# First unit's row maxima in two pairs, its loads ahead of two seed stores, and a third tile for evacuating q and k

## The chip, the cores and the metric

One core of one Trainium2 chip runs the whole program. The metric is the device time of one execution in microseconds, as the median of several runs; one further execution was recorded by the profiler, and all rows below are from that one.

## The reference

Two independent layers work on two inputs and their results stand side by side in the output (2048 rows, 448 + 448 columns).

```python
# A: a long convolution (S4D): kernel K from 256 complex modes per channel, applied by FFT
dt = exp(log_dt); A = -exp(log_A_real) + 1j * A_imag; C = (C_real + 1j * C_imag) * dt[:, None]
P = exp((A * dt[:, None])[:, :, None] * arange(2048))
K = 2.0 * einsum("dn,dnl->dl", C, P).real              # 448 channels
y = irfft(rfft(u, 4096) * rfft(K, 4096), 4096)[:2048] + u * D_skip
# B: full multi-head attention, 16 heads of 28, no mask
q, k, v = split_heads(x @ wqkv)                         # 2048 x 448 each
p = softmax(q @ k^T * 28 ** -0.5)                       # row maximum over all 2048 keys
b = (p @ v) @ wo
out = concatenate([y, b], axis=-1)
```

## The kernel before

The program has a first part of some 240 us and a long main loop. A wrapper records every instruction, so all instructions have line 75 in the profile, and one goes by tile names.

**First part.** Queries, keys and values are projected from `x` in four chunks `c` of 512 rows. `qk_proj(c, s, g)` computes keys (`s == 1`) or queries (`s == 0`) of a group `g` of four heads by 12 matmuls into one of three PSUM tiles `pm`. Its `evac` splits the result into a high part (ScalarE) and a low part (VectorE) in a tile `hl` (two buffers), and stores that to DRAM (`k_d`, `q_d`). The weights lie in the tile `khat` (`k0_t`) of the first group's keys, a quarter of the tile for each group of heads, so a quarter can be loaded with keys when its group's last projection is done. `work` holds the projections, `project()` emits one and the evacuation of the one before it.

Between the projections lie the seeds of layer A: for each of eight blocks `o` a list of 13 steps, `seeds(o)`, four slots apart, up to slot 41. They make the tables `se` (in a buffer of the ring `qhat`, three buffers, shared with the loaded queries) and `sg`. The steps that matter here, in their order: `sizes` (11 exponentials, ScalarE), `reduce` (VectorE), `sines` (ScalarE), `g_base` (GpSimd and ScalarE, tile `gz`), `places`/`e_base` (GpSimd, tile `qhat`), `e3` and `g_first` (VectorE), `e5` (GpSimd, six operations with `x_e`), `g_copies` (ScalarE), and two stores, `put_g` (1456 KB) and `put_e` (896 KB), from `sg` and `qhat` to `sd`.

Then come the row maxima of the first unit, 512 queries of four heads: 16 row tiles `i`, of each four matmuls against 512 columns. Columns 0 to 1023 are handled as a pair: `kdif` holds key differences of the two halves, ScalarE takes relu(q kdif) into `rl`, and VectorE adds the product with the second half and reduces to the maximum in one instruction (`tensor_tensor_reduce`, in the profile CUSTOM_DVE_ANT_0 and a short read). Columns 1024 to 2047 are two plain maxima (TENSOR_REDUCE). `max_join` and `max_end` join the maxima and transpose them, and `max_put` writes the negated maximum (tile `mh`) by two small DMAs into the rows 28 and 29 of the queries, where the main loop's scores take it as an added row.

**Order.** In the first part a scheduler orders each engine's instructions from emission order and its own costs; from the main loop on the emission order is kept. All loads and stores are issued from SyncE, in one order: an instruction that waits there holds all that follow. Each waits for the one eight places before it.

**Main loop.** It begins with three row tiles of the second unit's maxima (`LEAD = 3`, 12 matmuls), then steps through 256 steps: scores `pss`, exponential `p`, product with `v`, next maxima, the convolution's work in slots.

What the change touches: `A1` and `KW` (slots in which the loads of the first queries and keys are emitted), `hl`, `project()`, `max_mm`'s callers, `max_join`, the two last steps of `seeds(6)`.

Of the kernel before, what the change touches and what calls it, by code (L numbers as in the profile page):

```python
# [23 lines left out]
HG = H // G  # L24
CQ = 512
NQ = L // CQ
# [14 lines left out]
PS = 1  # L41
SGB, XB, XL = 2, 5, 4
K0, KP, KD, UP = 0, 3.5, 4, 3
A0, A1, KW = 26, 34, (33, 35, 36)

N1 = 32
N2 = 64
# [5 lines left out]
NO = 8  # L53
# [37 lines left out]
def body(ctx, tc, a, out):  # L91
    nc = Engines(tc)
# [39 lines left out]
    kd_p = pool(att, "kd_p", side="right")  # L132
    k0_p = pool(k0_st, "k0_p", side="right")
# [31 lines left out]
    def load_q(u, rows=range(4)):  # L165
        g, c = divmod(u, NQ)
        if 0 in rows:
            q_u[u] = q_p.tile([128, HG, CQ], F32R, name="qhat", bufs=3)
        t = q_u[u]
        for r in rows:  # L170
            nc.sync.dma_start(t[32 * r:32 * r + 32].bitcast(F32), q_d[g][c][r // 2].rearrange("(j p) q -> p j q", j=HG))

    def max_mm(u, i, kc, ps=w_tile):

        if i == 0 and kc == 0:
            m_u[u] = q_p.tile([128, HG, 4, 3], F32, name="mx", bufs=2)
        j, t = divmod(i, 4)
        pm = ps()
        q, kt = q_u[u][:, j, t * 128:(t + 1) * 128], kt_g[u // NQ][j]
        mx = m_u[u][:, j, t, max(kc - 1, 0):max(kc - 1, 0) + 1]  # L180
        if kc == 0:
            nc.tensor.matmul(pm, q, kd_g[u // NQ, j], start=True, stop=True)
            rl_u[u, i] = kd_p.tile([128, CQ], F32, name="rl", bufs=2)
            nc.scalar.activation(rl_u[u, i], pm, AF.Relu)
        elif kc == 1:
            kb = kt.rearrange("p (c s n) -> p c s n", c=NQ, s=2)[:, :2, 1, :]
            nc.tensor.matmul(pm.rearrange("p (c n) -> p c n", c=2), q, kb, start=True, stop=True)
            rl = rl_u.pop((u, i))
            nc.vector.tensor_tensor_reduce(rl, pm, rl, 1.0, -3.0e38, ALU.add, ALU.max, mx)
        else:  # L190
            nc.tensor.matmul(pm, q, kt[:, kc * CQ:(kc + 1) * CQ], start=True, stop=True)
            nc.vector.tensor_reduce(mx, pm, axis=AX.X, op=ALU.max)

    def max_join(u):
        m_u[u, 1] = q_p.tile([128, HG * 4], F32, name="m1", bufs=2)
        nc.vector.tensor_reduce(m_u[u, 1], m_u[u].rearrange("p a b c -> p (a b) c"), axis=AX.X, op=ALU.max)

    def max_end(u, ps):
        nc.tensor.transpose(ps[:16, :128], m_u[u, 1], ident)
        mh = q_p.tile([16, 2, 128], F32R, name="mh")  # L200
        nc.vector.tensor_scalar(mh[:, 0, :], ps[:16, :128], -1.0, None, op0=ALU.mult)
        nc.vector.scalar_tensor_tensor(mh[:, 1, :], ps[:16, :128], -1.0, mh[:, 0, :].bitcast(F32),
                                       op0=ALU.mult, op1=ALU.subtract)
        mh_u[u] = mh
# [7 lines left out]
    with ExitStack() as st:  # L212
# [3 lines left out]
        x_p = pool(xst, "x_p")  # L216
# [43 lines left out]
        t = a["A_log_dt"]  # L260
# [197 lines left out]
        def qk_proj(c, s, g):  # L458
            pp = w_tile()
            n = 0  # L460
            for k in range(NCK):
                for i, x_ in ((0, xh), (1, xh), (0, xl)):
                    nc.tensor.matmul(pp, w_g[:, i, s, k, g].rearrange("p h e -> p (h e)"), x_[k],
                                     start=n == 0, stop=n == 3 * NCK - 1)
                    n += 1

            def evac():
                hl = x_p.tile([128, 2, CQ], F32R, name="hl", bufs=2)
                th, tl = hl[:, 0], hl[:, 1]
                if s == 1:  # L470
                    nc.scalar.activation(th, pp, AF.Identity, bias=kones)
                    nc.vector.scalar_tensor_tensor(tl, pp, kones, th.bitcast(F32), op0=ALU.add, op1=ALU.subtract)
                else:
                    nc.scalar.activation(th, pp, AF.Copy)
                    nc.vector.tensor_tensor(tl, pp, th.bitcast(F32), ALU.subtract)
                if s == 1 and c < 2:
                    HC = CQ // 2
                    kb = y_p.tile([128, HC], F32, name="kb")
                    dhl = y_p.tile([128, 2, HC], F32R, name="dhl")
                    dh, dl = dhl[:, 0], dhl[:, 1]  # L480
                    nc.scalar.activation(kb, pp[:, HC:], AF.Copy)
                    nc.vector.tensor_tensor(kb, pp[:, :HC], kb, ALU.subtract)
                    nc.scalar.activation(dh, kb, AF.Copy)
                    nc.gpsimd.tensor_tensor(dl, kb, dh.bitcast(F32), ALU.subtract)
                    nc.sync.dma_start(kd_d[g][:, :, c * HC:(c + 1) * HC].rearrange("i p l -> p i l"), dhl.bitcast(F32))
                nc.sync.dma_start((k_d[g][:, :, c * CQ:(c + 1) * CQ] if s == 1 else q_d[g][c]).rearrange("i p l -> p i l"),
                                  hl.bitcast(F32))
            return evac
# [16 lines left out]
        work = []  # L505
# [8 lines left out]
        stages = [seeds(o) for o in range(NO)]  # L514
        n_stage = SP * (NO - 1) + len(stages[0])
        slots = [[] for _ in range(n_stage)]
        for o in range(NO):
            for i, st_ in enumerate(stages[o]):
                slots[max(SP * o + (i or -2), 0)] += st_
# [3 lines left out]
        ahead = collections.defaultdict(list)  # L523
# [2 lines left out]
        for i in range(2):  # L526
            ahead[A1 + i].append(lambda i=i: load_q(0, range(2 * i, 2 * i + 2)))

        for j, t in enumerate(KW):
            ahead[t].append(lambda j=j: load_k(0, j, k0_p))  # L530

        def project():

            e = work.pop(0)() if work else None
            while pend:
                pend.pop(0)()
            if e:
                pend.append(e)

        for t in range(n_stage):  # L540
            while work and n_work - len(work) < n_work * (t + 1) / PW:
                project()
            for f in slots[t] + ahead.get(t, []):
                f()
            if t + 1 == PW:
                project()
                wst.close()
                load_k(0, HG - 1, k0_p)
                load_q(1)
                for c in range(NQ):  # L550
                    load_v(0, c)
        xst.close()
        more = [lambda: ps_t.tile([128, CQ], F32, name="pt")] * 2 + [w_tile] * 3
        for i in range(16):
            for kc in range(4):
                max_mm(0, i, kc, more[(4 * i + kc) % 5])
        nc.scalar.activation(half_pi[:1], half_pi[:1], AF.Exp)
        max_join(0)
        max_end(0, ps_t.tile([128, CQ], F32, name="pt"))
        max_put(0)  # L560
        sst.close()
# [315 lines left out]
    for i in range(LEAD):  # L877
        for kc in range(4):
            max_mm(1, i, kc)
# [122 lines left out]
    last = [None]  # L1002
# [13 lines left out]
    for s in range(NS):  # L1016
        u, kt = divmod(s, NK)
# [24 lines left out]
        ps = []  # L1042
# [97 lines left out]
```

## Time and profile before

| | |
|---|---|
| median of 3 runs | 1292.87 us (1292.81 to 1293.53) |
| profiled execution, its time | 1296.34 us |
| its span, first to last instruction | 1294.3 us |
| mean granted TensorE clock | 0.976 |
| TensorE busy | 1228.1 us (95%) |
| VectorE, ScalarE, GpSimd busy | 933.2, 956.6, 847.0 us |
| moved by DMA | 205.36 MB, 159 GB/s on the mean |

The profiled execution is 3.5 us longer than the median run. Shares over the whole span say little of the first part; what the change touches runs in the first 250 us.

### The profile page before, as it was taken

Reading aid. Unit: us, or ns where it says so; the run is one execution under the profiler, and the core shown is the slowest. Engines: PE = TensorE matmul, PEld = TensorE weight load, DVE = VectorE, ACT = ScalarE, POOL = GpSimd, SP = SyncE. Lnnn points to the kernel's source line nnn. Section 1 sums busy time; section 2 is a strip of 40 time slices with the busy share of each in tenths; the row PEclk is TensorE's granted clock in tenths of the full one; section 3 lists DMA queues with packets and bytes.
Section 4 is the critical chain, followed back from the end, with each engine's and each line's share of the span. In section 5 each row is a group of like instructions: output and inputs, shape, how many; then the busy total and the mean of one; then the engine's idle time right before and its main releaser. Section 6 shows DMA issues by size and latency. Waiting matters only on the chain.

```text
span 1294.3 us, 33256 instructions
## 1 busy us (share of the span) xinstructions
PE 1228.1 (95%) x12625; PEld 703.1 (54%) x12625; DVE 933.2 (72%) x2106; ACT 956.6 (74%) x2142; POOL 847.0 (65%) x728
## 2 busy tenths in 40 slices
PE   7979885899999999999999999999999999999997
PEld 5767762455555555555555555555555555554433
DVE  5778876878777787787788888888888655645111
ACT  4878762488888888888888888888887766656552
POOL 2466571398888788888769999998996222424321
PEclk9889887899999999999999999999999999999999
DMA  6677779736765546468634132742425443647655
GB/s 193 229 261 253 245 235 289 210 73 145 181 147 137 125 139 166 131 164 237 177 95 111 48 87 52 164 108 68 103 51 155 154 152 133 202 151 243 201 163 169
DMA packets 200088, 205.36 MB, mean 159 GB/s; under 512 B 95992, under 2 KB 158520, under 8 KB 197880
## 3 DMA queue, kind: packets, MB, share of 16 engines
q1 hardware_dynamic: 199928, 203.23, 55.7%
q8 instruction: 100, 1.64, 0.5%
q14 instruction: 60, 0.49, 0.1%
HBM read 120.73 MB, written 82.18 MB: 157 GB/s over the span
## 4 chain that ended last, share of the span: by engine, by line
PE 76%; DVE 9%; POOL 5%; ACT 4%; issue 3%; DMA 3%; SPq 0%; ACTq 0%; POOLq 0%; DVEq 0%
PE pm L75 43%; PE pss L75 16%; PE po L75 16%; DVE mx L75 2%; ACT tri L75 1%; POOL e L75 1%; DVE rl L75 1%; DMA khat<-k 1%; POOL qhat L75 1%; DVE tri L75 1%; DVE px L75 1%; DVE sg L75 1%; DVE qhat L75 1%; POOL p L75 1%; PE pt L75 1%
## 5 line engine op out<-in xcount | busy, mean ns | idle before, releaser
L75 ACT ACTIVATE p<-pss 128x512 f32<-128x512 f32 x1024 | 561.2, 611 | 112.1 <-PE pss L75 107.6
L75 PE MATMUL pss<-qhat,khat 128*128 128x512 f32 x1024 | 403.1, 400 | 1.5 <-ACT p L75 1.4
L75 DVE TENSOR_REDUCE mx<-pm 128x1 f32<-128x512 f32 x500 | 321.7, 684 | 109.2 <-PE pm L75 107.0
L75 PE MATMUL pm<-khat,qhat 128*128 128x512 f32 x749 | 327.1, 440 | 3.3 <-DVE mx L75 2.1
L75 POOL TENSOR_TENSOR e<-e,sdb 128x256 f32<-128x256 f32 x168 | 201.9, 1202 | 118.6 <-ACT e L75 109.3
L75 PE MATMUL po<-p,v 128*32 128x512 f32 x2048 | 269.4, 594 | 0.0
L75 POOL TENSOR_TENSOR e<-e,eu 128x256 f32<-128x256 f32 x168 | 248.1, 1477 | 13.2
L75 PEld LDWEIGHTS pm<-khat,qhat 128*128 128x128 f32 x749 | 141.9, 190 | 199.1 <-ACT p L75 48.6
L75 DVE CUSTOM_DVE_ANT_0 rl<-pm,rl 128x512 f32<-128x512 f32 x249 | 171.5, 689 | 65.6 <-ACT rl L75 62.0
L75 PEld LDWEIGHTS pss<-qhat,khat 128*128 128x128 f32 x1024 | 190.7, 189 | 45.7 <-issue 10.8
L75 POOL TENSOR_TENSOR eu<-e,sdb 128x256 f32<-128x256 f32 x168 | 201.9, 1202 | 0.0
L75 POOL TENSOR_TENSOR p<-pr,pr 64x448 f32<-64x448 f32 x64 | 73.1, 1143 | 159.5 <-PE pm L75 134.0
L75 ACT ACTIVATE rl<-pm 128x512 f32<-128x512 f32 x249 | 151.2, 607 | 20.9 <-PE pm L75 20.9
L75 DVE TENSOR_TENSOR g<-g,zg 128x128 f32<-128x128 f32 x392 | 162.2, 414 | 3.4
L75 PE MATMUL pm<-xh,khat 112*128 112x512 f32 x256 | 90.3, 434 | 14.1 <-DVE hl L75 7.1
L75 PE MATMUL pm<-kdif,qhat 128*128 128x512 f32 x249 | 101.3, 407 | 2.4 <-DVE mx L75 1.3
L75 DVE TENSOR_TENSOR zg<-g,zg 128x128 f32<-128x128 f32 x224 | 87.9, 393 | 5.1
L75 PEld LDWEIGHTS pm<-e,g 128*32 128x32 f32 x3584 | 57.2, 109 | 43.8 <-issue 16.4
L75 DVE TENSOR_TENSOR pr<-pm,ub 128x448 f32<-128x448 f32 x64 | 37.0, 620 | 56.4 <-PE pm L75 42.0
L75 PE MATMUL pm<-e,g 128*32 128x64 f32 x3584 | 73.0, 222 | 1.9 <-POOL e L75 1.9
L75 ACT ACTIVATE y<-pm 128x448 f32<-128x448 f32 x48 | 26.5, 553 | 58.1 <-PE pm L75 34.0
L75 PEld LDWEIGHTS pm<-xh,khat 112*128 112x128 f32 x256 | 52.5, 209 | 29.0 <-DVE hl L75 8.6
(134 smaller groups left out, 1446.0 us busy)
## 6 DMA issues: line engine op xcount, KB each, us to landing
sdb<-sd SPq DMA_DIRECT2D x56, 336.0 KB
khat<-k SPq DMA_DIRECT2D x64, 256.0 KB
qhat<-q SPq DMA_DIRECT2D x64, 256.0 KB
sd<-sg SPq DMA_DIRECT2D x8, 1456.0 KB
k<-hl SPq DMA_DIRECT2D x16, 512.0 KB
q<-hl SPq DMA_DIRECT2D x16, 512.0 KB
mw<-in_mw SPq DMA_DIRECT2D x16, 512.0 KB
sd<-qhat SPq DMA_DIRECT2D x8, 896.0 KB
```

The costliest lines, as they stand in the source:

```text
L75: i = f(*args, **kw)
```

## The change

For columns 1024 to 2047 of the first unit, the two plain maxima become a second pair: TensorE adds q k2 and (-q) k3 in one PSUM tile (two matmuls), ScalarE takes the relu, and VectorE adds q k3 and reduces, as for the first pair. The negated queries `q_neg` are four ScalarE instructions of 128x512. Per row tile there are five matmuls instead of four, two ScalarE instructions instead of one, two VectorE pairs instead of one pair and two maxima.

The queries' load is emitted three slots earlier, the keys' loads inside `project()`. The stores `put_g` and `put_e` of `seeds(6)` are taken out of their slots: `put_e` is emitted behind the last keys' load and one load of values, `put_g` behind the loads of the second unit's queries and the other values. `hl` has three buffers.

```diff
-A0, A1, KW = 26, 34, (33, 35, 36)
+A0, A1 = 26, 31
+    def max_pair(i, kc, ps, q_neg):
+        j, t = divmod(i, 4)
+        ts = slice(t * 128, (t + 1) * 128)
+        pm, kt = ps(), kt_g[0][j]
+        if kc == 2:
+            nc.tensor.matmul(pm, q_u[0][:, j, ts], kt[:, 2 * CQ:3 * CQ], start=True, stop=False)
+            nc.tensor.matmul(pm, q_neg[:, j, ts], kt[:, 3 * CQ:], start=False, stop=True)
+            rl_u[0, i] = kd_p.tile([128, CQ], F32, name="rl", bufs=2)
+            nc.scalar.activation(rl_u[0, i], pm, AF.Relu)
+        else:
+            nc.tensor.matmul(pm, q_u[0][:, j, ts], kt[:, 3 * CQ:], start=True, stop=True)
+            rl = rl_u.pop((0, i))
+            nc.vector.tensor_tensor_reduce(rl, pm, rl, 1.0, -3.0e38, ALU.add, ALU.max, m_u[0][:, j, t, 1:2])
-    def max_join(u):
+    def max_join(u, n=3):
...
-                hl = x_p.tile([128, 2, CQ], F32R, name="hl", bufs=2)
+                hl = x_p.tile([128, 2, CQ], F32R, name="hl", bufs=3)
...
+        kept_g, kept_e = (stages[NO - 2][i] for i in (-2, -1))
+        stages[NO - 2][-2:] = []
...
-        for j, t in enumerate(KW):
-            ahead[t].append(lambda j=j: load_k(0, j, k0_p))
         def project():
-            e = work.pop(0)() if work else None
+            j, last = divmod(len(work) - 1, 2)
+            e = work.pop(0)() if work else load_k(0, HG - 1, k0_p)
             while pend:
                 pend.pop(0)()
             if e:
                 pend.append(e)
+            if e and not last and j < HG - 1:
+                load_k(0, HG - 2 - j, k0_p)
...
             if t + 1 == PW:
                 project()
                 wst.close()
-                load_k(0, HG - 1, k0_p)
+                load_v(0, 0)
+                kept_e.pop()()
                 load_q(1)
-                for c in range(NQ):
+                for c in range(1, NQ):
                     load_v(0, c)
+                kept_g.pop()()
...
+        q_neg = pool(n_st, "n_p").tile([128, HG, CQ], F32R, name="q_neg")
+        for j in range(HG):
+            nc.scalar.activation(q_neg[:, j], q_u[0][:, j].bitcast(F32), AF.Copy, scale=-1.0)
         for i in range(16):
             for kc in range(4):
-                max_mm(0, i, kc, more[(4 * i + kc) % 5])
+                f, kw = (max_mm, (0, i, kc)) if kc < 2 else (max_pair, (i, kc))
+                f(*kw, more[(4 * i + kc) % 5], *([q_neg] if kc > 1 else []))
...
-        max_join(0)
+        max_join(0, 2)
```

The built program of the changed kernel shows what its scheduler makes of this. On SyncE the order near the end of the first part becomes: first unit's queries, keys of quarter 0, store of q1 (queries of group 1, last chunk), store of k2, keys of quarter 1, stores of q2 and k3, keys of quarters 2 and 3, store of q3, values, `put_e(6)`, values, queries of the second unit, `put_g(6)`, `put_g(7)`, `put_e(7)`, and then the two small DMAs of `mh`. Before, it was: keys 0, store k2, queries, store q2, `put_g(6)`, queries, keys 1, store k3, `put_e(6)`, keys 2, store q3, keys 3, queries of the second unit, values, `put_g(7)`, `put_e(7)`, `mh`. ScalarE and VectorE get another order too: `e3(6)` and `g_first(6)` stand behind the sines of block 7 on VectorE, a multiplication of `g_base(7)` stands ahead of `e5(6)` on GpSimd, and on ScalarE the evacuation of k2 stands behind a copy that waits for GpSimd's `gz` of block 7; the evacuations of q2, k3 and q3 stand behind the first relu of the maxima.

More of the change, by code (lines that the diff above doesn't have):

```diff
@@ L192, in max_mm @@
             nc.vector.tensor_reduce(mx, pm, axis=AX.X, op=ALU.max)
-    def max_join(u):
+    def max_join(u, n=3):
         m_u[u, 1] = q_p.tile([128, HG * 4], F32, name="m1", bufs=2)
-        nc.vector.tensor_reduce(m_u[u, 1], m_u[u].rearrange("p a b c -> p (a b) c"), axis=AX.X, op=ALU.max)
+        nc.vector.tensor_reduce(m_u[u, 1], m_u[u].rearrange("p a b c -> p (a b) c")[:, :, :n], axis=AX.X, op=ALU.max)
     def max_end(u, ps):
@@ L547, in body @@
                 wst.close()
-                load_k(0, HG - 1, k0_p)
+                load_v(0, 0)
+                kept_e.pop()()
                 load_q(1)
-                for c in range(NQ):
+                for c in range(1, NQ):
                     load_v(0, c)
+                kept_g.pop()()
         xst.close()
         more = [lambda: ps_t.tile([128, CQ], F32, name="pt")] * 2 + [w_tile] * 3
+        n_st = ExitStack()
+        q_neg = pool(n_st, "n_p").tile([128, HG, CQ], F32R, name="q_neg")
+        for j in range(HG):
+            nc.scalar.activation(q_neg[:, j], q_u[0][:, j].bitcast(F32), AF.Copy, scale=-1.0)
         for i in range(16):
             for kc in range(4):
-                max_mm(0, i, kc, more[(4 * i + kc) % 5])
+                f, kw = (max_mm, (0, i, kc)) if kc < 2 else (max_pair, (i, kc))
+                f(*kw, more[(4 * i + kc) % 5], *([q_neg] if kc > 1 else []))
         nc.scalar.activation(half_pi[:1], half_pi[:1], AF.Exp)
-        max_join(0)
+        n_st.close()
+        max_join(0, 2)
         max_end(0, ps_t.tile([128, CQ], F32, name="pt"))
```

## The prediction

> **What bounds the kernel now.** I read the page first, then the first 260 us in windows, the order of time (timeline) around the first unit's maxima, the groups in that stretch, the waits, and the chain of waits.
>
> ```profile
> span 1294.3 us, 33256 instructions
> ...
> PE 1228.1 (95%) x12625; PEld 703.1 (54%) x12625; DVE 933.2 (72%) x2106; ACT 956.6 (74%) x2142; POOL 847.0 (65%) x728
> ...
> PE   7979885899999999999999999999999999999997
> ```
>
> TensorE is the bound, but not in the first eight slices of 32.4 us: digits 7, 9, 7, 9, 8, 8, 5, 8. From the ninth on it is full, and nothing there is changed. So the question is how much earlier the main loop's first score is computed; that shift goes to the end one to one. The seventh slice (194 to 227 us), the worst, is the first unit's maxima:
>
> ```profile
> 184.00:188.00 4.00, 1.31 (x3) 1.12 (x4) 2.01 (x4) 3.97 (x13) 3.47 (x8) 0.51 0.11 42
> ...
> 196.00:200.00 4.00, 0.00 (x0) 0.00 (x0) 2.41 (x5) 1.14 (x3) 2.53 (x3) 0.72 1.06 310
> ...
> 204.00:208.00 4.00, 1.06 (x3) 0.89 (x4) 0.00 (x0) 0.26 (x1) 0.00 (x0) 0.50 1.11 235
> ...
> 212.00:216.00 4.00, 3.11 (x10) 1.57 (x9) 3.69 (x9) 1.53 (x3) 0.00 (x0) 1.00 1.12 315
> ...
> 236.00:240.00 4.00, 1.66 (x5) 0.82 (x6) 3.38 (x9) 0.00 (x0) 0.00 (x0) 0.84 0.58 196
> ...
> 188.00:237.50 49.50, 32.18 (x86) 17.25 (x85) 36.27 (x79) 12.86 (x24) 6.64 (x8) 0.83 1.04 293
> ```
>
> Columns: PE, PEld, DVE, ACT, POOL busy, granted clock, DMA share, GB/s. Two things run side by side. VectorE is full from 208 on. And the DMA engines are full (share 1.04, 293 GB/s) from 188 to 237.5, after a nearly empty stretch (0.11). The order of time has the marks:
>
> ```profile
> 200.22 0.38 SPq L75 DMA_DIRECT2D k<-hl  x1
> ...
> 206.94 0.76 PE L75 MATMUL pt<-kdif,qhat 128*128 128x512 f32 x1 [12.47 <-DMA khat<-k]
> ...
> 239.91 1.27 SPq L75 DMA_DIRECT2D qhat<-mh  x2
> ...
> 246.80 0.63 PE L75 MATMUL pss<-qhat,khat 128*128 128x512 f32 x1
> ```
>
> The last key store (k3) is issued at 200.2, TensorE waits 12.5 us for loads until 206.9, the negated maxima `mh` are written at 239.9, the first score comes at 246.8.
>
> **The maxima by pairs.** What VectorE does from 206.9 to 238.8:
>
> ```profile
> L75 DVE TENSOR_REDUCE mx<-pm 128x1 f32<-128x512 f32 x20 | 13.1, 684 | 0.0
> L75 DVE TENSOR_REDUCE mx<-pt 128x1 f32<-128x512 f32 x12 | 8.0, 684 | 0.0
> L75 DVE CUSTOM_DVE_ANT_0 rl<-pm,rl 128x512 f32<-128x512 f32 x9 | 6.2, 685 | 1.2 <-PE pm L75 1.2
> L75 DVE CUSTOM_DVE_ANT_0 rl<-pt,rl 128x512 f32<-128x512 f32 x7 | 4.8, 683 | 5.1 <-ACT rl L75 5.1
> ...
> L75 ACT ACTIVATE rl<-pm 128x512 f32<-128x512 f32 x12 | 7.2, 598 | 19.7 <-PE pm L75 19.7
> ```
>
> Per row tile it does a pair (0.69) and two plain maxima (2 x 0.68): 2.05 us of durations. The stretch from 208.4 to 238.8 (30.4 us, 16 tiles) shows 1.9, as starts overlap ends a little. After: two pairs. With two `rl` buffers, relu and pair take turns: 0.60 + 0.69 and two hops, some 0.1 together, so 1.39 us per two pairs, 0.69 per pair; 32 pairs are 22.2 us. The phase gets 8 us shorter. TensorE then has five matmuls per tile:
>
> ```profile
> 239.56 7.44 PE pm L75 x13
> 247.43 0.43 PE pm L75
> 249.58 0.23 PE pm L75
> ```
>
> That is 5 x 0.23 = 1.2 us at full clock (under 1.39, hidden) and 5 x 0.43 = 2.15 at half clock (not hidden). Before, the clock was 1.00 from 212 on; I take full clock after the first few us. The four negations (about 0.6 each, by the relu row) lie on ScalarE ahead of the second relu: 2.4 us, mostly beside the last evacuations. The shorter join costs nothing.
>
> **The third `hl` tile.** What two buffers cost now (waits of 165 to 206 and of 60 to 100 us, the chain, and a window):
>
> ```profile
> ACT hl L75 <- DMA k<-hl: 6.5, 1, 6.5
> ...
> PE pm L75 <- DVE hl L75: 5.9, 1, 5.9
> ...
> 81.03 3.19 DMA q<-hl
> ...
> 80.00:100.00 20.00, 14.29 (x59) 12.08 (x60) 12.76 (x26) 14.30 (x34) 10.60 (x17) 0.74 0.88 303
> ```
>
> ScalarE waits 6.5 us for a key store to land before it can evacuate k3; near 80 TensorE stalls 5.9 us, and 3.2 us of a store's transfer are on the chain. Both waits go. Of the early one I keep 3 us (the chain's piece); between 0 (the seeds on VectorE, ScalarE and GpSimd are late next, which are busy 12.8, 14.3 and 10.6 of 20 us there) and 6. The scheduler's new order of the early seeds could also lose up to 3.
>
> **When the last keys are stored now.** This is the step on which the sum rests. Keys of quarters 2 and 3 stand behind the store of k3 in SyncE's order, so its issue time, T3, sets the rest. In the changed order k2's evacuation stands on ScalarE behind the copy of `gz(7)`; that waits for GpSimd, whose `e5(6)` now waits for the sines of block 7. I add it up from durations:
>
> ```profile
> 173.16 2.10 POOL L75 TENSOR_TENSOR qhat<-qhat 128x336 f32<-128x336 f32 x1 [3.22 <-DVE qhat L75]
> ...
> 180.72 1.21 POOL L75 TENSOR_TENSOR qhat<-qhat,x_e 128x336 f32<-128x336 f32 x1
> ...
> 172.79 1.28 ACT L75 ACT_TABLE_LOAD   x1 [2.20 <-DVE tri L75]
> 174.09 1.83 ACT L75 ACTIVATE tri<-pn 128x112 f32<-128x112 f32 x11
> ...
> 188.51 0.75 DVE L75 SCALAR_TENSOR_TENSOR hl<-pm,kones,hl 128x512 fp32r<-128x512 f32 x1 [1.46 <-ACT hl L75]
> ...
> L75 ACT ACTIVATE tri<-tri 128x1232 f32<-128x1232 f32 x16 | 19.9, 1242 | 0.1
> ...
> L75 POOL TENSOR_TENSOR qhat<-tri 128x112 f32<-128x112 f32 x48 | 20.9, 468 | 0.0
> L75 POOL TENSOR_TENSOR qhat<-qhat,x_e 128x336 f32<-128x336 f32 x16 | 19.9, 1241 | 0.6
> L75 POOL TENSOR_TENSOR x_e<-qhat 128x336 f32<-128x336 f32 x16 | 19.7, 1230 | 4.5 <-DVE qhat L75 3.9
> ...
> L75 ACT ACTIVATE hl<-pm,kones 128x512 fp32r<-128x512 f32 x16 | 11.3, 706 | 10.4 <-DMA k<-hl 7.9 <-PE pm L75 2.5
> ...
> L75 ACT ACTIVATE tri<-tri,half_pi 128x1232 f32<-128x1232 f32 x8 | 10.5, 1317 | 0.0
> ...
> L75 POOL TENSOR_TENSOR tri<-tri 128x224 f32<-128x224 f32 x8 | 7.9, 992 | 10.7 <-ACT tri L75 10.7
> L75 POOL TENSOR_TENSOR gz<-tri 128x224 f32<-128x224 f32 x8 | 7.5, 941 | 16.1 <-ACT tri L75 15.0 <-DVE px L75 1.0
> L75 DVE TENSOR_TENSOR qhat<-qhat 128x112 f32<-128x112 f32 x16 | 7.2, 480 | 2.4 <-POOL qhat L75 2.4
> ```
>
> The table load before block 7's exponentials starts at 172.8 now; I take 173.5, as VectorE's operations ahead of it change places. Then ScalarE: load 1.3, exponentials 1.8, k1 0.7, load 1.3, sine 1.2, q1 0.7, absolute value 1.2, sine 1.3: 183.0. GpSimd's multiplication 1.0: 184.0; what VectorE still owes to `e3(6)` is four operations of 0.48, 185.9; five operations of `e5(6)` at 1.23: 192.0; `gz` 0.9: 192.9. ScalarE's three copies (about 1.0) and k2's evacuation 0.7, VectorE's half 0.75: k2 is out at 195.4, against 189.3 now (188.51 + 0.75). That is the cost of the new order, 6 us; it also holds q3's matmuls, which wait for k2's PSUM tile. GpSimd: two fills and six products of block 7, under 3.5: 196.3. VectorE: `e3(7)` and `g_first(7)`, 14 operations of about 0.48: 203.0. Then q2, the first pair, k3 (0.75 + 0.69 + 0.75): 205.2. Less the 3 us gained early, T3 is 202.2, that is 2 us later than now (200.2), with a range of 196 to 208.
>
> **What is queued behind T3.** From k3's store on, DMA has to move, in MB: k3 0.52, two quarters of keys 2.10, q3 0.52, values 1.05, `put_e(6)` 0.92, queries 1.05, `put_g` of 6 and 7 2.98, `put_e(7)` 0.92: 10.06, at 293 GB/s 34.3 us. Moving the two stores back brings the keys ahead, but `mh` is behind both, and the first score needs `mh`. That the queue is served in order shows in the chain:
>
> ```profile
> 195.85 11.10 DMA khat<-k
> ```
>
> A 256 KB load is on the chain for 11.1 us, 0.9 us of which are its own bytes; the rest is what stood ahead. The small transfer needs some 2 us more (3.2 us was a 512 KB store in the chain's row), and the first block's seed table, loaded behind it, holds ScalarE's first exponential for about 1 us. So by the backlog the first score's place in the loop is at T3 + 36.3 + 1, 239.5. By the engines: the maxima go on from T3 + 1, 31 pairs of 0.69 are 21.4, join and transposition 1, then 12 matmuls of the second unit as now (7.4): T3 + 31, 233. The keys themselves land in time: quarters 2 and 3 within about 5 and 9 us of T3, needed 10 and 16 us after it. So the backlog is last, not VectorE: without the pairs the engines would be at 241, so of their 8 us only some 1.5 count. Gain: 246.8 - 239.5 = 7.3 us.
>
> Why it is any gain at all: now the engines were idle at 184 to 188 (share 0.11) and 49.5 us of full queue followed; after, the first keys and queries (2.1 MB, 7 us) are moved in that hole and before it.
>
> The Trainium skill, "DMA: Bandwidth & Descriptors", section "Queues, rings and completion order", says that an engine takes descriptors in ring order and that a transfer's completion is written after all earlier writes of that engine; by that rule `mh` waits for the whole backlog, as in my sum. The same section says that completion is not in issue order across engines when a copy uses only some of them; if `mh` did so, the time would be that of the first rival.
>
> **The rivals.**
> 1. The backlog doesn't hold `mh` (it finishes early, or the rate is that of a store, higher than the mean). Then the engines' path ends last, T3 + 31 = 233.2, gain 13.6: 1279.3. For it: VectorE was the full engine now. Against: the share of 1.04 until 237.5 with `mh` just behind.
> 2. Slower: the seeds' chain across three engines gets longer still. T3 is the sum of some 40 operations that wait for one another over GpSimd, VectorE and ScalarE. It decides from T3 = 209.5 on (209.5 + 37.3 = 246.8). If the early 3 us are lost instead of gained (6 us), and `e5(6)` takes the 8.8 us that it took in the trace from 173.2 to 181.9 (2 us more), T3 is 210; with 3 us more in block 7's operations 213, and the time is 1292.9 + 3.5 = 1296.4. For it: the new order has GpSimd waiting for the sines. Against: the evacuations no longer wait for stores.
> 3. TensorE stays at half clock in the maxima, with the short waits between its matmuls: 16 tiles at 2.15 are 34.4 us from T3 + 1, the first score at T3 + 1 + 34.4 + 8.4 = 246: no change, 1292. Against: 1.00 at 212 to 216 with TensorE busy 3.1 of 4 us.
>
> **How the numbers follow.** The profiled execution took 1296.34 for a span of 1294.3, the median run 1292.87; I subtract the shift from the median: 1292.9 - 7.4 = 1285.5 (by the profiled one, 1289). Chances: the backlog with T3 from 198 to 206, 0.52 (1281 to 1290); rival 1, 0.22 (1275 to 1283); rival 2, 0.18 (1290 to 1298); rival 3, 0.08. 0.2% is 2.6 us, about what a measurement of this kernel can tell from no change. Faster by more: the first two, and a little of the second rival, 0.76. Within: half of rival 2 and most of rival 3, 0.15. Slower by more: 0.09. The range leaves out some 0.06 below and 0.08 above: 1277 to 1294.
>
> **What would show it.** k3's store near 202 (not 198 or 210); ScalarE's evacuation of k2 right behind the `gz` copy, and GpSimd's `e5(6)` begun after 183; pairs 0.69 apart, the phase under 24 us; the DMA share near 1 until about 236, and a wait of the first score for DMA, with TensorE idle some 5 us before it. A first score right behind the second unit's matmuls, with no such wait, would show the first rival; a first score after 246.8 the second; matmuls of 0.43 throughout the maxima the third. The main loop should keep its length.

## The result, and the profile after

The changed kernel takes 1285.68 us in the median (1283.41 to 1286.97), the kernel before on the same chip 1293.13 (1292.81 to 1293.53): 7.4 us less, ratio 0.9941, 95% interval 0.9929 to 0.9953. The prediction was 1285.5. The number is nearly exact. Part of its working is not, and the experiments show that the gain comes from another part of the change than the prediction weighed most.

The page of the changed kernel: span, busy times, TensorE's busy share in 40 slices. Its profiled execution took 1284.56.

```profile
span 1282.7 us, 33325 instructions
...
PE 1223.2 (95%) x12641; PEld 699.9 (55%) x12641; DVE 925.3 (72%) x2106; ACT 967.7 (75%) x2162; POOL 842.6 (66%) x728
...
PE   7988867999999999999999999999999999999987
```

The order of time in the changed kernel, around the last key stores and the first score:

```profile
164.48 1.28 ACT L75 ACT_TABLE_LOAD   x1 [2.62 <-DVE tri L75]
...
173.76 0.99 POOL L75 TENSOR_TENSOR tri<-tri 128x224 f32<-128x224 f32 x1 [11.05 <-ACT tri L75]
...
176.33 1.02 POOL L75 TENSOR_TENSOR qhat<-qhat 128x336 f32<-128x336 f32 x1 [1.59 <-DVE qhat L75]
...
184.34 0.39 ACT L75 ACTIVATE gz<-gz 128x224 f32<-128x224 f32 x1 [3.50 <-POOL gz L75]
...
184.98 0.65 ACT L75 ACTIVATE hl<-pm,kones 128x512 fp32r<-128x512 f32 x1
...
185.67 0.75 DVE L75 SCALAR_TENSOR_TENSOR hl<-pm,kones,hl 128x512 fp32r<-128x512 f32 x1 [3.34 <-ACT hl L75]
...
186.48 1.22 PE L75 MATMUL pm<-xh,khat 112*128 112x512 f32 x2 [11.25 <-DVE hl L75]
...
196.00 0.38 SPq L75 DMA_DIRECT2D k<-hl  x1
...
198.51 0.69 DVE L75 CUSTOM_DVE_ANT_0 rl<-pm,rl 128x512 f32<-128x512 f32 x1 [1.94 <-ACT rl L75]
...
222.64 0.69 DVE L75 CUSTOM_DVE_ANT_0 rl<-pm,rl 128x512 f32<-128x512 f32 x1 [0.34 <-ACT rl L75]
...
224.36 2.45 SPq L75 DMA_DIRECT2D qhat<-mh  x2
...
232.60 0.80 PE L75 MATMUL pss<-qhat,khat 128*128 128x512 f32 x1 [1.38 <-DMA qhat<-mh]
...
233.03 0.42 ACT L75 ACTIVATE e<-sdb 128x256 f32<-128x256 f32 x1 [3.46 <-DMA sdb<-sd]
```

And the windows (columns as in the prediction):

```profile
192.00:196.00 4.00, 1.24 (x3) 0.82 (x3) 2.46 (x6) 3.50 (x9) 2.12 (x3) 0.71 0.49 119
...
204.00:208.00 4.00, 3.55 (x14) 1.96 (x12) 3.19 (x10) 2.59 (x5) 0.00 (x0) 1.00 1.02 211
...
220.00:224.00 4.00, 2.04 (x9) 0.97 (x7) 2.85 (x11) 1.69 (x3) 0.00 (x0) 1.00 1.05 345
...
196.00:236.00 40.00, 34.41 (x98) 19.67 (x98) 29.48 (x82) 23.15 (x45) 2.33 (x4) 0.80 1.00 298
...
224.00:228.00 4.00, 4.00 (x8) 1.83 (x8) 3.08 (x9) 1.19 (x2) 0.00 (x0) 0.55 1.06 389
...
228.00:232.00 4.00, 3.22 (x6) 1.44 (x5) 3.18 (x8) 0.60 (x1) 0.00 (x0) 0.50 1.09 377
...
236.00:240.00 4.00, 4.00 (x17) 1.96 (x17) 3.16 (x10) 2.59 (x5) 3.84 (x4) 0.74 0.95 221
```

What ends last before the main loop is what the prediction said, by 1.4 us: a DMA queue that is full from k3's store (196.0) to 236 (mean share 1.00, 298 GB/s), with `mh` near its end. The first score waits for `mh`, and ScalarE's first copy waits for the seed table behind it. The first score moved from 246.80 to 232.60, by 14.2 us. The medians differ by only 7.4. So two things were open: where the other 7 us went, and which part of the change brings the gain.

### The profile page after: what moved, and what is told of

Read it like the earlier page. It is cut to its first block, busy times and chain, and to the rows that moved or that the text cites. A ratio compares the mean times of both kernels' runs of the same rounds, so it can differ in the third digit from the quotient of the medians.

```text
span 1282.7 us, 33325 instructions
## 1 busy us (share of the span) xinstructions
PE 1223.2 (95%) x12641; PEld 699.9 (55%) x12641; DVE 925.3 (72%) x2106; ACT 967.7 (75%) x2162; POOL 842.6 (66%) x728
## 4 chain that ended last, share of the span: by engine, by line
PE 75%; DVE 7%; DMA 6%; POOL 4%; ACT 3%; issue 3%; SPq 1%; POOLq 0%; ACTq 0%; DVEq 0%
PE pm L75 43%; PE pss L75 16%; PE po L75 15%; DMA ut<-in_A_u 2%; POOL e L75 1%; SPq L75 1%; DMA khat<-k 1%; DVE mx L75 1%; ACT tri L75 1%; DVE hl L75 1%; DVE sg L75 1%; DMA v<-v 1%; DMA sd<-qhat 1%; POOL p L75 1%; POOL qhat L75 1%
## 5 line engine op out<-in xcount | busy, mean ns | idle before, releaser
L75 DVE TENSOR_REDUCE mx<-pm 128x1 f32<-128x512 f32 x480 | 308.7, 684 | 110.1 <-PE pm L75 107.8
L75 DVE CUSTOM_DVE_ANT_0 rl<-pm,rl 128x512 f32<-128x512 f32 x259 | 178.3, 689 | 71.4 <-ACT rl L75 69.4
L75 ACT ACTIVATE rl<-pm 128x512 f32<-128x512 f32 x259 | 156.8, 607 | 10.9 <-PE pm L75 10.6
L75 PE MATMUL pm<-xh,khat 112*128 112x512 f32 x256 | 87.1, 422 | 21.0 <-DVE hl L75 12.2
L75 PEld LDWEIGHTS pm<-e,g 128*32 128x32 f32 x3584 | 57.3, 109 | 43.8 <-issue 16.6
L75 PEld LDWEIGHTS pm<-xh,khat 112*128 112x128 f32 x256 | 49.9, 200 | 35.0 <-DVE hl L75 13.5
```

What stands on the lines that cost most here:

```text
L75: i = f(*args, **kw)
```

## The experiments

The kernel before, on the same chip beside each of them, has medians of 1292.5 to 1293.3. Each T3, "maxima" and "score" is a moment of one profiled execution. T3 is the issue of k3's store, as in the prediction; "maxima" is the start of the join behind the last pair, "score" the first score, from each kernel's order of time.

| kernel | median | ratio, 95% interval | T3 | maxima | score | score − T3 |
|---|---|---|---|---|---|---|
| before (page in the prediction) | 1292.87 | | 200.22 | 238.84 | 246.80 | 46.6 |
| before, second profile | 1292.82 (one run) | | 196.54 | 235.19 | 243.16 | 46.6 |
| third tile alone | 1284.87 | 0.9940, 0.9925–0.9954 | 189.14 | 227.62 | 235.33 | 46.2 |
| third tile, pairs | 1282.75 | 0.9919, 0.9905–0.9934 | 188.50 | 224.24 | 232.21 | 43.7 |
| the same, stores of block 6 moved | 1281.82 | 0.9909, 0.9895–0.9923 | 188.47 | 221.10 | 230.78 | 42.3 |
| the same, four `rl` tiles | 1279.45 | 0.9899, 0.9885–0.9912 | 186.55 | 219.79 | 227.85 | 41.3 |
| the same (two `rl`), small loads on ScalarE's queue | 1280.82 | 0.9908, 0.9894–0.9922 | 186.82 | 219.79 | 229.99 | 43.2 |
| changed | 1285.68 | 0.9941, 0.9929–0.9953 | 196.00 | 223.38 | 232.60 | 36.6 |
| changed, again | 1285.12 | 0.9943, 0.9928–0.9959 | 195.54 | 223.93 | 232.38 | 36.8 |
| changed without pairs | 1287.52 | 0.9955, 0.9941–0.9969 | 200.35 | 231.22 | 238.92 | 38.6 |
| changed, stores back at their places | 1288.67 | 0.9970, 0.9959–0.9980 | 194.82 | 223.12 | 235.23 | 40.4 |
| changed with two `hl` tiles | 1292.38 | 1.0001, 0.9990–1.0012 | 203.21 | 233.81 | 241.46 | 38.3 |
| changed, four `rl` tiles | 1285.73 | 0.9944, 0.9932–0.9956 | 198.29 | 226.86 | 234.66 | 36.4 |
| changed, `mh` on ScalarE's queue | 1283.27 | 0.9927, 0.9915–0.9939 | 198.53 | 225.60 | 234.92 | 36.4 |

**The kernel before, profiled again.** No edit.

> The kernel before, unchanged, profiled a second time. The first score came 14.2 us earlier in the changed kernel's profile (246.80 to 232.60), the medians of the runs differ by 7.45 only, and the profile of before was 3.2 us above its median. If those 3 us lie ahead of the first score, a profile near the median (1292 to 1294) has its first score near 243.6 and the same main loop; if they lie in the main loop, the first score is again at 246 to 247 and the rest of the span is 3 us shorter. Either way 1292 to 1297.

Its span is 1290.8. One window, one of SyncE's waits (176 to 198 us), and the order of time:

```profile
180.00:184.00 4.00, 1.18 (x3) 0.99 (x4) 2.01 (x4) 3.97 (x13) 3.34 (x8) 0.55 0.07 29
...
SPq L75 <- DVE hl L75: 6.5, 1, 6.5
...
166.31 0.38 SPq L75 DMA_DIRECT2D k<-hl  x1
...
193.24 0.69 ACT L75 ACTIVATE hl<-pm,kones 128x512 fp32r<-128x512 f32 x1 [6.85 <-DMA k<-hl]
...
196.54 0.38 SPq L75 DMA_DIRECT2D k<-hl  x1
...
243.16 0.63 PE L75 MATMUL pss<-qhat,khat 128*128 128x512 f32 x1
```

The first answer: T3 and the first score are 3.7 and 3.6 us earlier than in the first profile, and the stretch between them is the same 46.6. The first profile was late ahead of T3 only. A chunk's key store that stands at 111.56 here stood at 114.63 there, so most of it was lost by then. Against this profile the changed kernel's first score is 10.6 us earlier, its span 8.1 us shorter. The other 2.5 us lie behind the first score: from it to the first evacuation of `ko` are 15.0 us here (243.16 to 258.16), 16.6 in the changed kernel (232.60 to 249.24), and the rest of the span is 0.9 longer there.

**The third tile alone.**

```diff
-                hl = x_p.tile([128, 2, CQ], F32R, name="hl", bufs=2)
+                hl = x_p.tile([128, 2, CQ], F32R, name="hl", bufs=3)
```

> Before, with the third tile for evacuating q and k alone: no pairs in the second half of the keys, loads and stores in the old order. Theory (the stores of the key chunks set the start of the maxima, and the third tile alone brings them forward): k3's store 4 to 6 us ahead of 200.2, so 194 to 196; the maxima, VectorE's 30 us, and the first score follow by as much, time 4 to 6 us under before (1287 to 1289). Rival (the queue is the bound from 188 on, and the two seed stores ahead of the key loads hold the first pair wherever k3's store is): k3's store earlier, the first pair and the first score not, time within 1.5 us of before.

The same window as above, and the order of time:

```profile
180.00:184.00 4.00, 3.79 (x10) 2.98 (x11) 3.63 (x10) 0.41 (x1) 1.51 (x3) 0.57 0.98 235
...
179.75 0.66 ACT L75 ACTIVATE hl<-pm,kones 128x512 fp32r<-128x512 f32 x1
...
185.95 0.60 ACT L75 ACTIVATE hl<-pm 128x512 fp32r<-128x512 f32 x1 [5.53 <-DMA k<-hl]
...
189.14 0.38 SPq L75 DMA_DIRECT2D k<-hl  x1
...
235.33 0.39 PE L75 MATMUL pss<-qhat,khat 128*128 128x512 f32 x1
```

One number in one line brings 8.2 us, as much as the whole change. Against the second profile of before, T3 is 7.4 us earlier, the maxima and the first score 7.6 and 7.8. The theory holds, at more than the size expected (4 to 6).

The wait for k3 is not where most of it comes from. k3 is evacuated at 179.75 instead of 193.24, by 181.4 with both halves, but its store is issued only at 189.1: the 9.0 us between the stores of k2 and k3 are filled for 7.6 us by SyncE's own rows, the loads of queries and keys above all. Of the 7.4 us at T3, 2.2 are there at the last chunk's first key store (166.31 to 164.07) and 6.5 at k2's store (186.71 to 180.18). In between lies SyncE's wait of 6.5 us in the kernel before: it has to store q1, ScalarE starts the evacuation of q1 only at 180.49, and meanwhile the DMA engines run empty (share 0.07 from 180 to 184). With three tiles ScalarE starts it at 172.33, that wait is gone, and the share is 0.98. So the third tile by itself fills the empty stretch which the prediction wanted to fill with loads. Whether it does so through the free tile or through the order that the scheduler makes with it, the run does not separate. The wait for a store to land is still there (5.53), but it falls on q3.

**The change without the third tile.**

```diff
-                hl = x_p.tile([128, 2, CQ], F32R, name="hl", bufs=3)
+                hl = x_p.tile([128, 2, CQ], F32R, name="hl", bufs=2)
```

> The changed kernel with two tiles for evacuating q and k. Theory (the third tile is most of the gain: in the kernel before it was worth 8.2 us alone): ScalarE waits again for stores to land, T3 is 200 to 204, the first score 235 to 240, time 3 to 7 us over the changed kernel (1289 to 1293). Rival (in the new order the copy of gz holds k2's evacuation, and the tile adds nothing late): only the early 2 to 3 us are lost, T3 198 to 199, time 1287 to 1288.5.

```profile
198.92 0.69 ACT L75 ACTIVATE hl<-pm,kones 128x512 fp32r<-128x512 f32 x1 [4.00 <-DMA k<-hl]
...
203.21 0.38 SPq L75 DMA_DIRECT2D k<-hl  x1
```

T3 is 203.2, and nothing of the gain is left: ratio 1.0001, 0.9990 to 1.0012. The pairs and the new order together bring nothing without the third tile. The first score, 241.46, is 1.5 us past the upper end expected. This is the mirror of the run before it, and SyncE's waits are too: from 170 to 205 us it waits 16.6 us for evacuations, against 6.3 in the changed kernel, and the DMA share falls to 0.00 from 192 to 196.

**The pairs.** Two runs: the change with the maxima as before, and the pairs with the third tile in the old order of loads and stores.

```diff
-                f, kw = (max_mm, (0, i, kc)) if kc < 2 else (max_pair, (i, kc))
-                f(*kw, more[(4 * i + kc) % 5], *([q_neg] if kc > 1 else []))
+                max_mm(0, i, kc, more[(4 * i + kc) % 5])
...
-        max_join(0, 2)
+        max_join(0)
```

> The changed kernel with the maxima as before (one pair and two plain maxima per row tile); third tile and order of loads kept. By the prediction's sum from the measured T3 of 196.0: engines' path T3 + 1 + 30.4 + 1 + 7.4 = 236, the backlog's place 232.6 unchanged; so the engines are last and 3 us are lost: first score 235 to 237, time 2.5 to 4.5 us over the changed kernel. Rival A (the backlog decides, and pairs are worth nothing): first score 232 to 233, time the same within 1. Rival B (the pairs are the gain, some 6 us): first score 238 to 240.

```diff
+A0, A1, KW = 26, 34, (33, 35, 36)
...
+        for j, t in enumerate(KW):
+            ahead[t].append(lambda j=j: load_k(0, j, k0_p))
...
-                load_v(0, 0)
-                kept_e.pop()()
+                load_k(0, HG - 1, k0_p)
                 load_q(1)
-                for c in range(1, NQ):
+                for c in range(NQ):
                     load_v(0, c)
-                kept_g.pop()()
```

> Pairs and third tile, but loads and stores in the order of before: the seed stores of blocks 6 stand ahead of the last two quarters of the keys. It shows what the new order is worth. The prediction's reason is that mh waits for the whole backlog in either order, as the bytes ahead of it are the same (10.06 MB); the order only lets the first keys and queries be moved in the hole near 192. By that: T3 near 195, keys land later, the pairs wait for them, first score 234 to 237, time 2 to 4 us over the changed kernel. Rival (the order buys nothing, since the new order delays k2's evacuation by as much): first score 231 to 233, time the same within 1. Rival (the order is the main gain): first score 238 and more, time 5 or more over the changed kernel.

In the changed kernel the pairs are worth 2.0 us of the place of the first score (38.6 against 36.6 after T3); the medians differ by 1.8 to 2.4, under the 2.5 to 4.5 expected, and their intervals overlap. (The first score itself, 238.92, is where the rival of 6 us put it, but T3 is 4.4 us later in that execution, and the pairs come behind it.) On the third tile alone they are worth 2.5 of the place (46.2 against 43.7) and 2.1 of the median; these intervals overlap too. So both rivals of the first run (nothing; 6 us) fall by the place, which both comparisons give alike; the medians alone would not settle it. The second run's time missed all three expected cases: the old order is not slower and not equal, but some 2.4 to 2.9 us faster than the change (the intervals of the two ratios just overlap). Its first score (232.21) and its mechanism are those of the rival "the order buys nothing". The order of time shows it:

```profile
174.12 0.37 ACT L75 ACTIVATE gz<-gz 128x224 f32<-128x224 f32 x1
...
178.24 0.66 ACT L75 ACTIVATE hl<-pm,kones 128x512 fp32r<-128x512 f32 x1
...
188.50 0.38 SPq L75 DMA_DIRECT2D k<-hl  x1
...
232.21 0.63 PE L75 MATMUL pss<-qhat,khat 128*128 128x512 f32 x1
```

The copy of `gz` is at 174.12 here, at 184.34 in the changed kernel, k2's evacuation at 178.24 against 184.98, and T3 at 188.50 against 196.00. The new order delays the keys by 7.5 us, and brings the loads forward by about as much: the first score comes 7.1 us sooner after T3 (36.6 against 43.7). It buys back what it costs, less 0.4, and the start of the main loop behind it is 1.5 us longer (16.6 against 15.1 to `ko`). In the second run nothing waits for `mh`; there the engines are last.

**Which part of the new order delays the keys.** The change has two: the loads of keys and queries at new places, and the stores of block 6 behind them. Each was put back by itself.

```diff
-        kept_g, kept_e = (stages[NO - 2][i] for i in (-2, -1))
-        stages[NO - 2][-2:] = []
...
-                kept_e.pop()()
...
-                kept_g.pop()()
```

> The changed kernel with the two stores of block 6 back at their places, the loads of keys and queries at the new ones. Theory (the loads' new places delay the seeds): T3 195 to 197 as in the changed kernel; the keys behind 2.4 MB more, about 7 us, the maxima start or stall up to 4 us later; first score 232 to 237, time 0 to 4 us over the changed kernel. Rival (the moved stores delay the seeds): T3 188 to 190, first score 231 to 233, time 2 to 3 us under it.

T3 stays at 194.8: the moved stores are not what delays the seeds. The time is 3 to 3.5 us over the change, near the upper end, and the place is 40.4 after T3:

```profile
226.31 1.28 SPq L75 DMA_DIRECT2D qhat<-mh  x2
...
235.23 0.76 PE L75 MATMUL pss<-qhat,khat 128*128 128x512 f32 x1 [4.26 <-DMA qhat<-mh]
```

`mh` now stands behind three seed tables as well (336 KB each, 1.03 MB in all, 3.5 us at 298 GB/s), and the first score moves by 3.8 (40.4 against 36.6). That agrees with the backlog theory: with a megabyte more ahead of `mh`, the first score is later by its transfer. It is no clean test, as the stores of block 6 stand elsewhere too.

The other half: loads at their old places, stores behind them.

```diff
+        kept_g, kept_e = (stages[NO - 2][i] for i in (-2, -1))
+        stages[NO - 2][-2:] = []
...
                 load_k(0, HG - 1, k0_p)
+                load_v(0, 0)
+                kept_e.pop()()
                 load_q(1)
-                for c in range(NQ):
+                for c in range(1, NQ):
                     load_v(0, c)
+                kept_g.pop()()
```

> Pairs and third tile with the loads of keys and queries at their places of before, and only the two stores of block 6 moved behind them. In the build the order of ScalarE's evacuations stays that of the kernel with pairs and third tile alone, so by the theory (the loads' new places, not the moved stores, delay the seeds of block 6 and with them k3's store, by 7 us) T3 is 188 to 189, nothing of the 2.3 MB seed stores is ahead of keys and queries, the first pair is at 190 to 192 instead of 196.65, engines' path to the first score 27.6 + 8 after it: 226 to 228, the backlog's place T3 + 36.6 = 225. First score 226 to 229, time 1278 to 1281. Rival A (the moved stores delay the seeds): T3 near 196, first score 232 or later, time 1284 to 1287. Rival B (the stores ahead of the keys cost nothing): first score 231 to 233, time 1282 to 1284.

```profile
222.09 2.78 SPq L75 DMA_DIRECT2D qhat<-mh  x2
...
230.78 0.80 PE L75 MATMUL pss<-qhat,khat 128*128 128x512 f32 x1 [1.84 <-DMA qhat<-mh]
...
231.11 0.42 ACT L75 ACTIVATE e<-sdb 128x256 f32<-128x256 f32 x1 [3.83 <-DMA sdb<-sd]
```

T3 is 188.47, as without the moved stores: the loads' new places are what delays the seeds, shown from both sides. Over all profiles with three tiles, T3 is 186.6 to 189.1 in the five with the old places and 194.8 to 200.4 in the six with the new ones. The maxima end 3.1 us sooner than with the stores ahead of the keys, as expected; but the first score, expected at 226 to 229, is at 230.8 and waits for `mh`. The backlog's place was taken from T3 (36.6 after it), and that was wrong: bytes not yet moved at T3 count too. Here the DMA engines are full at that moment, where the changed kernel has its empty stretch (0.49 from 192 to 196) just before it:

```profile
188.00:192.00 4.00, 0.00 (x0) 0.00 (x0) 2.64 (x6) 1.12 (x4) 1.02 (x1) 0.50 1.09 273
```

The median, 1281.82, can't be told from 1282.75. But the loads' new places now have a price. The changed kernel differs from this one in nothing else, and is 3.3 to 3.9 us slower, with intervals apart. With the stores in their slots in both, new places against old are 1288.67 against 1282.75, 5.9 us, intervals apart as well. The moved stores gain some 3 to 3.5 us where the loads are at the new places, and no more than 0.9 where they are not.

**Two limits taken away from the changed kernel.** First `mh` on a queue of its own:

```diff
-    def max_put(u):
+    def max_put(u, dma=nc.sync.dma_start):
         for i in range(2):
-            nc.sync.dma_start(
+            dma(
...
-        max_put(0)
+        max_put(0, nc.scalar.dma_start)
```

> The changed kernel with the two small stores of mh issued by ScalarE, on its own queue, instead of SyncE's. Theory (mh waits for SyncE's queue of stores and loads): on the other queue it lands 1 to 3 us after its issue at T3 + 28.4, and the first score comes right behind the second unit's matmuls, with no wait for DMA: T3 + 35.2 instead of T3 + 36.6; but ScalarE's first exponential still waits for the seed table behind the same queue, so the time is lower by 0 to 1.4 only. Rival (the DMA engines are shared and mh waits for what stands ahead on whatever queue): the first score waits for mh as in the changed kernel, same time. Rival (the issue itself costs ScalarE more than it brings): 0.5 to 2 us slower.

```profile
226.60 1.70 ACTq L75 DMA_DIRECT2D qhat<-mh  x2
...
234.92 0.40 PE L75 MATMUL pss<-qhat,khat 128*128 128x512 f32 x1
...
235.44 0.42 ACT L75 ACTIVATE e<-sdb 128x256 f32<-128x256 f32 x1 [1.99 <-DMA sdb<-sd]
```

Its waits from 222 to 236 (who waited for whom: total, times, longest):

```profile
ACT rl L75 <- issue: 3.5, 1, 3.5
...
PE pm L75 <- ACT rl L75: 2.3, 3, 1.9
```

The DMA engines are as full as before (share 1.06 from 224 to 236), and the first score no longer waits for `mh`: it follows the second unit's matmuls. So `mh` waited for its queue, not for full engines. The Trainium skill ("DMA: Bandwidth & Descriptors", section "Queues, rings and completion order") says that each DMA engine takes turns between the queues that have work; this trace agrees. The score's place, 36.4 against the 35.2 expected, hardly moves: ScalarE takes 1.7 us for the two issues, its relu stands behind them, and TensorE waits up to 1.9 us for that, so the engines' path grows by about what the queue had cost. The median is 1.9 us lower; the intervals overlap.

Then four tiles for relu's output, in the changed kernel and in the faster order:

```diff
-            rl_u[0, i] = kd_p.tile([128, CQ], F32, name="rl", bufs=2)
+            rl_u[0, i] = n_p[0].tile([128, CQ], F32, name="rn", bufs=4)
```

> The changed kernel with four buffers for relu's output in the pairs. Theory (in the changed kernel the store and load queue behind k3's store is last, mh waits for it): the maxima may end 2 to 3 us sooner, mh is written sooner, the first score stays at 232 to 233.5 and the time within 1.3 us of the changed kernel. Rival (VectorE's maxima are last): first score 229 to 230.5 and 2 to 3 us gained.

> The same, with four buffers for relu's output in the first unit's pairs instead of two. If the two buffers make the 0.8 us per pair, the pairs come 0.70 apart, the phase is 32 x 0.1 = 3 us shorter, the engines' path ends at 223 to 225 and the backlog (225) is last: first score 225 to 227, time 1 to 3 us under the same kernel with two. If TensorE's five matmuls or the PSUM tiles make the 0.8, nothing changes.

In the changed kernel the time is the same (1285.73) and the place too (36.4). The pairs are no denser: in the faster order the third pair of VectorE starts at 196.26 and the last, the 32nd, at 219.06, which is 22.8 / 29 = 0.79 us each. So the two tiles don't make the 0.8, and the run on the changed kernel, in which the maxima did not get shorter, tests nothing of the backlog. The median of 1279.45, the lowest of all, is in the range expected, but not for the reason given: it comes with a T3 that was 1.9 us earlier, and its interval overlaps that of the same kernel with two tiles.

**Both small loads on ScalarE's queue, in the faster order.** The edit is that of `mh` above, and:

```diff
-        nc.sync.dma_start(sds[b], sd_d[b // BO][b % BO])
+        (nc.scalar if b < 3 else nc.sync).dma_start(sds[b], sd_d[b // BO][b % BO])
```

> Pairs, third tile, old places of the loads, stores of block 6 behind them, and mh and the first three seed tables on ScalarE's queue. There mh was issued at 222.1 and landed at 230.8, the seed table at 231.1, while the second unit's matmuls ended near 229. If the queue alone holds both, the first score is at 228.5 to 229.5 and the first exponential at 229.3 to 230.3 instead of 232.1: 1.5 to 2.5 us under that kernel, 1279 to 1280.5. If the main loop's next loads (queries, ua) stand behind the same queue and give it back: first exponential as said, time within 0.7 of 1281.8.

```profile
220.79 1.24 ACTq L75 DMA_DIRECT2D qhat<-mh  x2
...
222.07 1.56 ACTq L75 DMA_DIRECT2D sdb<-sd  x3
...
223.67 0.60 ACT L75 ACTIVATE rl<-pm 128x512 f32<-128x512 f32 x1 [4.64 <-issue]
...
224.32 0.80 PE L75 MATMUL pm<-khat,qhat 128*128 128x512 f32 x1 [3.02 <-ACT rl L75]
```

Both waits for DMA are gone, and another is in their place: ScalarE issues five DMAs in 2.8 us, its relu stands behind them, and TensorE waits 3.0 us for that. The first score comes 43.2 after T3 instead of 42.3; no gain can be told (1280.82 against 1281.82; the two cases expected were 1279 to 1280.5 and within 0.7 of 1281.8).

**The changed kernel again**, beside the last three:

> The changed kernel again, beside the three below. The early part differs by 2 to 4 us from one execution to the next (k3's store at 196.5 and 200.2 in two profiles of before), what follows k3's store does not: T3 194 to 199, first score at T3 + 36 to 38, median 1284.5 to 1286.5.

1285.12, with T3 at 195.54 and the score 36.8 later, as expected. Its profiled span, 1286.9, is 4.2 us over the first one's though the first score is 0.2 earlier: from `ko` on it takes 1038.2 us instead of 1033.5. Other profiles have 1032 to 1034 there, but for the run with the stores put back (1038.1). What makes these few microseconds is open.

## Why the prediction was right, step by step

**The backlog holds the first score: right, by a small margin, and its exact size is in part luck.** T3 + 37.3 was predicted, T3 + 36.6 and 36.8 measured; 293 GB/s predicted, 298 measured. On a queue of its own `mh` is no longer waited for, and a megabyte more ahead of it goes with 3.8 us. The first rival, that the backlog does not hold `mh`, falls. But 6 us over the engines' path were predicted, and 1.4 and 0.6 measured: the engines come in almost at the same time, so with `mh` off that queue (and ScalarE paying for it) the place was still T3 + 36.4. The engines' path was mis-sized: `mh` is written 28.4 us after T3, not 23.4. A pair takes 0.80 us (198.51 to 222.64, 30 intervals), not 0.69; four buffers did not change it. In the groups ScalarE and TensorE wait for each other:

```profile
L75 DVE CUSTOM_DVE_ANT_0 rl<-pm,rl 128x512 f32<-128x512 f32 x19 | 13.0, 690 | 5.0 <-ACT rl L75 4.9
...
L75 ACT ACTIVATE rl<-pm 128x512 f32<-128x512 f32 x19 | 11.0, 596 | 5.7 <-PE pm L75 5.4
```

By these rows, the step "relu and pair take turns" left out the matmul between a freed PSUM tile and the next relu; no run changed the number of those tiles. And the first pair of the steady run came 2.5 us after T3, not 1.

**T3 is 2 us later than now, 202.2: the moment is wrong, the chain is right.** T3 is 196.0, and 195.5 the second time (198.3 and 198.5 in the runs with four `rl` tiles and with `mh` on ScalarE's queue, whose edits touch only the maxima and `mh`). The step that failed is the start of the walk. The table load before block 7's exponentials was put at 173.5, less the 3 us gained early: 170.5. It is at 164.48. Of these 6.0 us, 3.8 are the lateness of the first profile of before, which has this load at 172.79, the second at 168.99. The other 2.2 are within what executions differ by: 163.3 to 167.0 in the six profiles with three tiles and the loads at the new places. The walk itself holds: from this load to the copy of `gz` 19.4 us were predicted and 19.9 measured, and from there to T3 12.3 and 11.7. GpSimd waits 11.05 us for the sines and begins `e5(6)` behind VectorE's part, as predicted, only at 176.33 and not after 183. k2's evacuation stands behind the copy of `gz`, and q3's matmuls wait 11.25 us for its PSUM tile. The 3 us gained early agree with the last chunk's first key store (166.31 in the second profile of before, 163.64 after), but that is no more than executions differ by.

**The baseline, and the main loop's length: wrong, the other way.** 200.2, the T3 from which "2 us later" was counted, belonged to an execution that was late by 3.7 us at that point, while the shift was subtracted from the median. (The sum gave 7.3; 7.4 was subtracted.) And the first score's shift did not go to the end one to one: of 10.6 us (against the second profile) 1.6 are lost at the start of the loop and 0.9 behind it. So the working gave 7.3 as T3 + 2 and a place 9.3 us nearer; measured are T3 − 0.5 and a place 10.0 nearer, less 2.5. The misses cancel to within a microsecond. So the exactness of the number is luck.

**What the gain is put down to: half wrong.** The prediction gave the third tile 3 us early, let the late wait of 6.5 us vanish in the walk, and explained the gain by loads moved into the empty stretch. The runs give the third tile 8.2 us by itself, and it fills the empty stretch without any load moved. They give the pairs some 2. The new order as a whole costs 2.4 to 2.9, with intervals that just overlap; the loads' new places alone cost 3.3 to 5.9, with intervals apart. That only some 1.5 us of the pairs' 8 count was right (2.0 to 2.5). The second rival, the longer chain of seeds, describes a true cost: T3 is 7.5 us later than in the old order with the same tile, about what the tile brings there (196.54 to 188.50). It never came near the 209.5 at which it would decide. The third, half clock in the maxima, did not happen: 1.00 from 204 to 224.

## What to carry to other kernels

When a change has several parts, price each alone against the same baseline before netting them: here one buffer brought the whole gain, and a reordering beside it gave part of it back without showing in the total. Before you subtract a predicted moment from a measured one, ask whether the profiled execution stands at the median at that very point; if it is late, it is late at some stage, and a second profile tells at which. A place taken as "so long after a store's issue" holds only as long as the bytes still queued at that moment are the same.

## What was not expected of the hardware

- An engine pays for the DMAs that it issues: five issues by ScalarE took 2.8 us, and its queued relu waited for them.
- The granted clock behind the maxima: 0.50 to 0.55 from 224 to 236 in the changed kernel, though TensorE is shown busy 3.2 to 4.0 of 4 us. With the third tile alone, where the first score waits for nothing, it is back at 1.00 from 236 to 240, against 0.74 in the changed kernel. That fits the 1.6 us lost at the start of the loop, but no run separates it from the late loads. The window of the third tile alone, a wait of the second unit's tiles in the changed kernel, and the group of the same weight loads in the first unit's maxima:

```profile
236.00:240.00 4.00, 4.00 (x21) 2.22 (x20) 3.79 (x12) 3.76 (x9) 3.84 (x4) 1.00 0.74 166
```

```profile
230.43 0.29 PEld L75 LDWEIGHTS pm<-kdif,qhat 128*128 128x128 f32 x1 [0.53 <-DVE mx L75]
```

```profile
L75 PEld LDWEIGHTS pm<-khat,qhat 128*128 128x128 f32 x26 | 4.5, 191 | 6.3 <-ACT rl L75 6.0
```

The Trainium skill ("TensorE: Matmul & The Clock Gate", section "A second HAM failure mode: psum-queue depth-cycling") describes a kernel that goes through PSUM banks in turn, idles briefly between groups of matmuls, and whose clock goes down and up by that. The rows don't decide whether this is such a case: the second unit's weight loads wait 0.3 to 0.5 us at a time, and the clock is at 0.50 to 0.55; the first unit's maxima wait as long (6.3 us over 26 loads, up to 0.66 at a time) and kept 1.00.
- Executions of one kernel differ by up to 3.7 us before the main loop (T3 of 196.54 and 200.22), and the stretch from T3 to the first score repeats to within 0.3 us (46.58 and 46.62; 36.60 and 36.84).
